# Three score buffers and four term buffers instead of two and five, with the second transpose in bf16 instead of 32-bit

## The chip, the cores and the metric

The kernel runs on one core of a Trainium2 chip. The engines are TensorE (PE, with its weight loads shown as PEld), VectorE (DVE), ScalarE (ACT), GpSimd (POOL) and SyncE (SP), which issues the DMAs. The metric is device time in microseconds of one execution. The median of the kernel before is 1739.27 us, of three runs from 1738.40 to 1739.86 us.

## The reference

Two layers follow each other, with the same weights in both. Each layer is an attention block and a token-mixing MLP, both with a residual:

```python
x = x + _A_ref(_layernorm(x, axis=-1), A_wqkv, A_wo)
x = x + _B_ref(_layernorm(x, axis=-1), B_w1, B_b1, B_w2, B_b2)
x = x + _A_ref(_layernorm(x, axis=-1), A_wqkv, A_wo)
x = x + _B_ref(_layernorm(x, axis=-1), B_w1, B_b1, B_w2, B_b2)
```

x has 2048 tokens of 640 features in bf16. `_A_ref` projects to q, k and v of 32 heads of 20 features, takes a softmax over all 2048 keys of the scores times 20 ** -0.5, multiplies by v and projects with wo. `_B_ref` normalises each token once more and works across tokens: w1 takes the 2048 tokens to 1536, then bias, GELU (tanh form), and w2 takes 1536 back to 2048, with a bias.

## The kernel before

**Attention.** The 32 heads are taken in 8 groups of 4 (`NG`), the queries in 4 blocks of 512, the keys in 16 tiles of 128. A unit is one query block, one head group and one key tile: 512 units a layer, 64 chunks of scores for each (query block, group) pair, which is called a segment. A chunk is the 128 x 512 scores of one head; four of them make a unit. The score matmuls (line 700) use four row tiles of PE, one for each head. The exponential of a chunk is taken in one of two ways:

- ScalarE (`do_exp`, line 887) reads two or three chunks at once from PSUM and writes `P` in bf16. There are four buffers of it (`NP_BUFS`).
- VectorE (`do_J` and `do_T`) makes exp2 out of integers. `do_J` (line 840) scales one chunk from PSUM into 16-bit integers in a buffer `J` that holds the four chunks of a unit. From that buffer `do_T` (line 860) makes five integer terms, each a halving with another constant, which read as bf16 are pieces of the exponential. Their sum is made by PE, which multiplies each of the five terms with v. A term buffer (`TT`) holds one term of one unit, 2048 values in each partition.

The multiplication with v (line 927) uses four column tiles of PE, and adds up over a segment in bank 6 of PSUM. One extra column of v is 1, so that the sums of the softmax come with it.

**Buffers.** `NJ_BUFS` = 2 buffers J and `NT_BUFS` = 5 buffers TT lie one behind the other in one region `JT` of 7 x 4096 bytes in each partition. A J buffer is taken by the first chunk of a unit and is given back when the fifth term has been made; a TT buffer is given back when PE has read its four chunks. In the first query block the last two TT buffers (`NTSV`) are held by saved partial sums, and `begin` leaves the other three free.

**Normalising a segment** (`normalize`). VectorE transposes the sums out of PSUM in blocks of 32 x 32 (line 976, 512 elements of 32 bits), takes the reciprocal of the sums (line 988), GpSimd multiplies (line 1001) into bf16, and VectorE transposes back (line 1011) into `attnT`. Before the change the multiply interleaves pairs of blocks, so that the transpose back moves 256 elements of 32 bits, each a pair of bf16. The output projection (`outproj`, line 1065) undoes the interleaving in the way that it reads its weights: four column tiles of 32 weights with a step of 2.

The last segment of a layer is computed in two halves of 256 queries, which are not interleaved.

**Output projection.** In query blocks 0 to 2 it is made when all 8 groups are there. In the last block it is made in parts: groups 0 to 5 after group 5, then 6 and 7 after group 7. The first part adds the residual into `x1last` (line 1094), a later part adds to it (line 1104).

**What sets the order.** The whole order on every engine is written while the program is built, by a planner. It keeps a clock for each engine, durations for each instruction (such as 600 ns for line 840, 605 for line 860, 720 for line 976), and rings of buffers with the time at which each is free. At each step it lets the engine with the earliest possible piece of work take it. `d_take` gives a unit to VectorE only if a J buffer is to be had and VectorE's clock would be through with it before ScalarE's. Other matmuls (projections, first MLP matmul, output projection) are fills between the attention's matmuls. On the chip each engine runs its instructions in that order and waits for semaphores.

Of the kernel before, what the change touches and what calls it, by code (L numbers as in the profile page):

```python
# [12 lines left out]
F32 = mybir.dt.float32  # L13
# [10 lines left out]
NG = 8  # L24
# [20 lines left out]

TERM_C = term_constants()
NP_BUFS = 4
NJ_BUFS = 2
NT_BUFS = 5
NA_BUFS = 10  # L50
NQ_BUFS = 9
NEARLY0 = 4
# [74 lines left out]
def kernel(  # L127
# [509 lines left out]
    def make_attention(L):  # L637
# [330 lines left out]
        def normalize(qb, g, half, src, ready, from_acc):  # L968
# [4 lines left out]
            def f_tr(start):  # L973
# [1 line left out]
                T1 = sb("T1", [128, w], F32, s1)  # L975
                nc.vector.transpose(out=T1[:], in_=src[:, 0:w])  # L976
                if from_acc:
                    acc["ready"] = start + 720 + LAT_V
                else:
                    sv_open[0] -= 1  # L980
                    if sv_open[0] == 0:
                        for i in range(NT_BUFS - NTSV, NT_BUFS):
                            rTT.give(i, start + 600)
                T1v = T1[:].rearrange("p (c i) -> p c i", i=32)

                def f_rec(start):
                    rden = stat.tile([128, 16], F32, name="rden")[:, 0:w // 32]
                    nc.vector.reciprocal(out=rden, in_=T1v[:, :, DH])  # L988

                    def f_mul(start):  # L990
                        s2 = rT2.take()
                        T2 = sb("T2", [128, w // 32, 32], BF16, s2)
                        eng = nc.vector if final else nc.gpsimd
                        end_ = start + (600 if final else 1450)
                        o_, a_, b_ = T2[:], T1v, rden.unsqueeze(2).to_broadcast([128, w // 32, 32])
                        if half is None:

                            o_ = o_.rearrange("p c i -> p (c i)").rearrange("p (c i b) -> p c b i", b=2, i=32)
                            a_ = T1[:].rearrange("p (c b i) -> p c b i", b=2, i=32)
                            b_ = rden.rearrange("p (c b) -> p c b", b=2).unsqueeze(3).to_broadcast([128, w // 64, 2, 32])  # L1000
                        eng.tensor_tensor(out=o_, in0=a_, in1=b_, op=ALU.mult)  # L1001
                        rT1.give(s1, end_)

                        def f_tr2(start):
                            if (qb, g) not in attnT:
                                aslot[(qb, g)] = rA.take()
                                attnT[(qb, g)] = sb("attnT", [128, 512], BF16, aslot[(qb, g)])
                            o_, i_ = attnT[(qb, g)][:, q0:q1], T2[:].rearrange("p c i -> p (c i)")
                            if half is None:
                                o_, i_ = o_.bitcast(F32), i_.bitcast(F32)  # L1010
                            nc.vector.transpose(out=o_, in_=i_)  # L1011
                            rT2.give(s2, start + 340)
                            on_normal(qb, g, half, start + 340 + LAT_V)
                        push("DVE", 3, end_, 340, f_tr2, ok=lambda: len(rA) > 0 and L.v_left[1] == 0)
                    if final:
                        push("DVE", 0, start + 150, 600, f_mul, ok=lambda: len(rT2) > 0)
                    else:
                        push("POOL", 0, start + 150 + LAT_V, 1300, f_mul, ok=lambda: len(rT2) > 0)
                push("DVE", 1, start + 720, 170, f_rec)
            push("DVE", 0, ready, 720, f_tr, ok=lambda: len(rT1) > 0)  # L1020

        def on_normal(qb, g, half, ready):
            if qb == LASTQB and g == NG - 3 or qb != LASTQB and g == NG - 1:
                for ttl in range(4):
                    load_xin(qb * 4 + ttl)
            if qb == LASTQB:
                gs = {NG - 3: list(range(NG - 2)), NG - 1: [NG - 2, NG - 1]}.get(g)
                if gs:
                    for ttl in range(4) if half is None else (2 * half, 2 * half + 1):
                        for ci in range(2):  # L1030
                            outproj(qb, gs, ttl, ci, ready, partial=True)
            elif g == NG - 1:
                for ttl in range(4):
                    for ci in range(2):
# [11 lines left out]
        def outproj(qb, gs, ttl, ci, ready, partial):  # L1046
# [8 lines left out]
            mms = []  # L1055
            for gi, gg in enumerate(gs):
                def mm(t, gg=gg, gi=gi):
                    at_ = attnT[(qb, gg)]
                    for c in range(4):
                        n = 4 * ttl + c  # L1060
                        if qb == LASTQB and gg == NG - 1:
                            q_ = at_[:, 32 * n:32 * n + 32]
                        else:
                            q_ = at_[:].rearrange("p (c i b) -> p c b i", b=2, i=32)[:, n // 2, n % 2]
                        nc.tensor.matmul(t[32 * c:32 * c + 32, 0:w], lhsT=q_, rhs=wo_pad[:, gg, c0:c1], start=(gi == 0),  # L1065
                                         stop=(gi == len(gs) - 1), tile_position=(0, 32 * c))
                mms.append(mm)

            def on_start(s):
# [39 lines left out]
            def when():  # L1109
# [1 line left out]
            add_fill(mms, 136.0, evac, 65 + 1.05 * w, ready=when if first else ready, pr=NU - NKT + 1 if final else (qb * NG + gs[-1] + 2) * NKT,  # L1111
                     urgent=qb >= LASTQB - 1, on_start=on_start, after=after,
                     ok=(lambda: tt in xin and (partial and L.mm1_left[0] == 0 or not partial and ("ds" in tt_state[tt] or len(rXD) > 0))) if first
                     else (lambda: n_part.get((tt, ci), 0) == 1))

        L.acc, L.pv, L.unassigned, L.pv_total, L.pv_done, L.d_count = acc, pv, unassigned, pv_total, pv_done, d_count
        L.opt_SA, L.do_SA, L.opt_SD, L.do_SD, L.do_PV, L.pv_ready, L.acc_open = opt_SA, do_SA, opt_SD, do_SD, do_PV, pv_ready, acc_open
# [556 lines left out]
```

## Time and profile before

| | us |
|---|---|
| median of three runs | 1739.27 |
| time of the profiled execution | 1739.86 |
| its span | 1738.1 |
| PE busy | 1660.4 (96%) |
| ScalarE busy | 1590.3 (91%) |
| VectorE busy | 1463.7 (84%) |
| GpSimd busy | 183.2 (11%) |

Busy time is the time in which at least one instruction of the engine ran. In the lists of groups each line has the source line, the engine, the operation, the tile written and read, the shapes, how often, then busy time and mean duration in ns, then how long the engine was idle just before such instructions and what ended that. The granted clock of TensorE is 0.994 over the span. The attention of layer 0 ends at about 803 us and that of layer 1 at about 1663 us; in both, query block 1 starts where VectorE makes the ninth first transpose of the layer (239 and 1096 us), block 2 at 422 and 1280 us, block 3 at 613 and 1470 us.

### The profile page before, as it was taken

What the parts mean: (1) busy time and instruction counts of PE and PEld (TensorE: products, weight loads), DVE (VectorE), ACT (ScalarE), POOL (GpSimd) and SP (SyncE); (2) the same over time, 40 slices, a digit from 0 to 9 for tenths busy, and PEclk for the clock granted to TensorE, in tenths of its full rate; (3) what the DMA queues carried; (4) which work ended last, traced back from release to release, by engine and by line L of the source; (5) the groups of instructions that cost most, each with busy time, mean ns of one, the idle gap of its engine ahead of it and who ended that gap; (6) DMA issues with size and microseconds to landing.
All of it is one profiled execution on the core that took longest, in us unless ns stands there. A gap on an engine that the chain in (4) does not pass through costs nothing.

```text
span 1738.1 us, 50479 instructions
## 1 busy us (share of the span) xinstructions
PE 1660.4 (96%) x21922; PEld 640.6 (37%) x21923; DVE 1463.7 (84%) x2613; ACT 1590.3 (91%) x1436; POOL 183.2 (11%) x297
## 2 busy tenths in 40 slices
PE   8999999999999999998999999999999999999989
PEld 3433333323333333335545423332233333333356
DVE  6588999999988889997444699999999888889963
ACT  7899999999999999997598799999999999999950
POOL 3100002000300021001101000210002000300010
PEclk9999999999999999999999999999999999999999
DMA  3200001000121105610522000100002120266133
GB/s 118 29 2 2 2 13 36 1 1 2 52 70 56 38 32 178 191 47 28 162 84 68 15 2 2 39 24 2 2 19 69 56 64 24 78 192 198 63 99 96
DMA packets 103295, 98.06 MB, mean 56 GB/s; under 512 B 45600, under 2 KB 79520, under 8 KB 103072
## 3 DMA queue, kind: packets, MB, share of 16 engines
q1 hardware_dynamic: 99456, 94.82, 17.7%
q8 instruction: 171, 2.80, 0.7%
q0 software_dynamic: 3616, 0.01, 0.3%
q14 instruction: 52, 0.43, 0.1%
HBM read 63.35 MB, written 31.46 MB: 55 GB/s over the span
## 4 chain that ended last, share of the span: by engine, by line
PE 48%; ACT 21%; DVE 19%; issue 9%; DMA 2%; POOL 1%; DVEq 0%; POOLq 0%; SPq 0%; ACTq 0%
ACT P L887 21%; PE pst L700 14%; PE pst L927 13%; PE pst L456 12%; DVE JT L860 7%; DVE JT L840 6%; PE pst L453 5%; PE pst L1065 3%; DVE T_85 L976 1%; PE pst L1483 1%; DMA W<-in_B_w_dram 1%; DVE attnT L1011 1%; DVE QT L463 0%; DMA uacc_74<-W 0%; DVE xs L1094 0%
## 5 line engine op out<-in xcount | busy, mean ns | idle before, releaser
L887 ACT ACTIVATE P<-pst 128x1536 bf16<-128x1536 f32 (+1 forms) x1336 | 1523.5, 1294 | 31.4 <-PE pst L700 15.3
L860 DVE TENSOR_SCALAR JT<-JT 128x2048 uint16<-128x2048 uint16 x945 | 636.0, 706 | 3.9 <-PE pst L927 0.2
L700 PE MATMUL pst<-QT,KT 32*128 32x512 bf16 (+1 forms) x4224 | 589.8, 376 | 36.3 <-ACT P L887 26.5
L840 DVE TENSOR_SCALAR JT<-pst 128x512 uint16<-128x512 f32 x756 | 504.0, 678 | 81.1 <-PE pst L700 78.2
L927 PE MATMUL pst<-P,Vaug 128*32 128x512 bf16 (+1 forms) x3444 | 503.9, 380 | 3.7 <-ACT P L887 1.9
L927 PE MATMUL pst<-JT,Vaug 128*32 128x512 bf16 (+1 forms) x3900 | 464.0, 379 | 4.9 <-DVE JT L860 2.4
L700 PEld LDWEIGHTS <-KT 32*128 32x128 bf16 x4224 | 165.5, 91 | 504.5 <-issue 492.8
L927 PEld LDWEIGHTS <-Vaug 128*32 128x32 bf16 x7344 | 170.9, 94 | 307.1 <-issue 275.6
L1001 POOL TENSOR_TENSOR T_86<-T_85,rden 128x512 bf16<-128x512 f32 x64 | 67.7, 1057 | 1157.1 <-DVE rden L988 1114.9
L1065 PE MATMUL pst<-wo,attnT 128*32 128x320 bf16 x2048 | 108.1, 304 | 7.1 <-DVE attnT L1011 3.9
L1483 PE MATMUL pst<-ident,zw 128*32 128x512 bf16 (+1 forms) x352 | 113.5, 374 | 0.0
L456 PEld LDWEIGHTS <-W 128*32 128x32 bf16 x3384 | 91.0, 96 | 59.8 <-issue 27.7
L456 PE MATMUL pst<-hh,wq 128*32 128x512 bf16 x1232 | 102.2, 381 | 2.2 <-DVE JT L840 1.7
L456 PE MATMUL pst<-hh,wk 128*32 128x512 bf16 x1240 | 95.2, 381 | 1.3 <-DVE JT L840 0.6
L456 PE MATMUL pst<-x1last,W 128*32 128x320 bf16 x1536 | 81.5, 301 | 0.8 <-DVE JT L840 0.4
L1065 PEld LDWEIGHTS <-attnT 128*32 128x32 bf16 x2048 | 51.7, 96 | 49.1 <-issue 26.8
L456 PE MATMUL pst<-attnT,hh 128*32 128x320 bf16 x1196 | 61.4, 300 | 2.5 <-DVE JT L840 0.8
L456 PE MATMUL pst<-JT,W 128*32 128x320 bf16 x1080 | 51.8, 300 | 0.0
L456 PE MATMUL pst<-hh,W 128*32 128x320 bf16 x768 | 43.2, 304 | 5.1 <-DMA W<-in_B_w_dram 3.7
L463 DVE CAST KT<-pst 128x512 bf16<-128x512 f32 x51 | 34.7, 679 | 15.9 <-PE pst L456 14.6
L976 DVE STREAM_TRANSPOSE T_85<-pst 128x512 f32<-128x512 f32 (+1 forms) x58 | 39.9, 688 | 7.0 <-PE pst L927 7.0
L354 POOL TENSOR_SCALAR rt<-mv 128x1 f32<-128x1 f32 x64 | 13.0, 203 | 310.9 <-DVE mv L346 309.9
(92 smaller groups left out, 878.3 us busy)
## 6 DMA issues: line engine op xcount, KB each, us to landing
W<-in_B_w_dram SPq DMA_DIRECT2D x10, 768.0 KB
W<-in_B_w_dram SPq DMA_DIRECT2D x24, 256.0 KB
xs<-in_A_x_dram SPq DMA_DIRECT2D x32, 160.0 KB
x2d<-xs SPq DMA_DIRECT2D x16, 320.0 KB
xs<-x2d SPq DMA_DIRECT2D x16, 320.0 KB
x1d_69<-xs SPq DMA_DIRECT2D x12, 320.0 KB
uacca_72<-W SPq DMA_DIRECT2D x12, 320.0 KB
W<-uacca_72 SPq DMA_DIRECT2D x12, 320.0 KB
```

Source lines behind the costliest of these rows:

```text
L453: nc.tensor.matmul(out_, lhsT=lhsT, rhs=rhs, start=start, stop=stop)
L456: nc.tensor.matmul(out_[32 * c:32 * c + 32], lhsT=lhsT[:, 32 * c:32 * c + 32], rhs=rhs, start=start, stop=stop, tile_position=(0, 32 * c))
L463: nc.vector.tensor_copy(out=out_, in_=in_)
L700: pe(nc.tensor.matmul(dst, lhsT=k_, rhs=q_, start=True, stop=True, tile_position=(32 * j, 0)))
L840: nc.vector.tensor_scalar(out=c["jt"][:, j * 512:(j + 1) * 512], in0=Dt[:], scalar1=SCALE * LOG2E * 256.0, scalar2=127.0 * 256.0, op0=ALU. ...
L860: nc.vector.tensor_scalar(out=tt_[:], in0=c["jt"][:], scalar1=0.5, scalar2=TERM_C[i], op0=ALU.mult, op1=ALU.add)
L887: nc.scalar.activation(out=P[:, 0:n, :].rearrange("p a b -> p (a b)"), in_=St[:, 0:n, :].rearrange("p a b -> p (a b)"), func=ACT.Exp, scal ...
L927: pe(nc.tensor.matmul(dst, lhsT=Vaug[:, n:n + 32], rhs=ap, start=acc["cnt"][j] == 1 and not part, stop=last[j] and (half is None or part = ...
L976: nc.vector.transpose(out=T1[:], in_=src[:, 0:w])
L1001: eng.tensor_tensor(out=o_, in0=a_, in1=b_, op=ALU.mult)
L1065: nc.tensor.matmul(t[32 * c:32 * c + 32, 0:w], lhsT=q_, rhs=wo_pad[:, gg, c0:c1], start=(gi == 0), stop=(gi == len(gs) - 1), tile_position ...
L1483: pe(nc.tensor.matmul(dst[0:32, 0:128 * n], lhsT=zw[:, 0:32], rhs=ident[:].unsqueeze(1).to_broadcast([128, n, 128]), start=not inside, sto ...
```

## The change

Two things change.

First, one of the five TT buffers becomes a third J buffer. The region keeps its size. A unit's chunks can be scaled while two older units still wait for terms; one term fewer can wait for PE. In the first query block the saved sums leave two TT buffers free where they left three.

Second, the interleaving is gone. The multiply writes its blocks in order, the transpose back moves 512 bf16 elements, and the output projection reads dense weights, with one full matmul where attention is over and four column tiles where it isn't. The durations that the planner reckons with are 600 and 150 ns for the first transpose and the reciprocal (720 and 170 before) and 400 ns for the transpose back (340 before). And in the last query block the output projection is made in four parts of two groups each (after groups 1, 3, 5 and 7) instead of two parts of six and two groups; the residual's tiles are loaded after group 1 instead of group 5.

```diff
 NP_BUFS = 4
-NJ_BUFS = 2
-NT_BUFS = 5
+NJ_BUFS = 3
+NT_BUFS = 4
...
                 if from_acc:
-                    acc["ready"] = start + 720 + LAT_V
+                    acc["ready"] = start + 600 + LAT_V
...
-                        o_, a_, b_ = T2[:], T1v, rden.unsqueeze(2).to_broadcast([128, w // 32, 32])
-                        if half is None:
-
-                            o_ = o_.rearrange("p c i -> p (c i)").rearrange("p (c i b) -> p c b i", b=2, i=32)
-                            a_ = T1[:].rearrange("p (c b i) -> p c b i", b=2, i=32)
-                            b_ = rden.rearrange("p (c b) -> p c b", b=2).unsqueeze(3).to_broadcast([128, w // 64, 2, 32])
-                        eng.tensor_tensor(out=o_, in0=a_, in1=b_, op=ALU.mult)
+                        eng.tensor_tensor(out=T2[:], in0=T1v,
+                                                in1=rden.unsqueeze(2).to_broadcast([128, w // 32, 32]), op=ALU.mult)
...
-                            o_, i_ = attnT[(qb, g)][:, q0:q1], T2[:].rearrange("p c i -> p (c i)")
-                            if half is None:
-                                o_, i_ = o_.bitcast(F32), i_.bitcast(F32)
-                            nc.vector.transpose(out=o_, in_=i_)
-                            rT2.give(s2, start + 340)
-                            on_normal(qb, g, half, start + 340 + LAT_V)
-                        push("DVE", 3, end_, 340, f_tr2, ok=lambda: len(rA) > 0 and L.v_left[1] == 0)
+                            nc.vector.transpose(out=attnT[(qb, g)][:, q0:q1], in_=T2[:].rearrange("p c i -> p (c i)"))
+                            rT2.give(s2, start + 400)
+                            on_normal(qb, g, half, start + 400 + LAT_V)
+                        push("DVE", 3, end_, 400, f_tr2, ok=lambda: len(rA) > 0 and L.v_left[1] == 0)
...
-                push("DVE", 1, start + 720, 170, f_rec)
-            push("DVE", 0, ready, 720, f_tr, ok=lambda: len(rT1) > 0)
+                push("DVE", 1, start + 600, 150, f_rec)
+            push("DVE", 0, ready, 600, f_tr, ok=lambda: len(rT1) > 0)
...
-            if qb == LASTQB and g == NG - 3 or qb != LASTQB and g == NG - 1:
+            if qb == LASTQB and g == 1 or qb != LASTQB and g == NG - 1:
...
-                gs = {NG - 3: list(range(NG - 2)), NG - 1: [NG - 2, NG - 1]}.get(g)
-                if gs:
+                if g % 2 == 1:
...
-                            outproj(qb, gs, ttl, ci, ready, partial=True)
+                            outproj(qb, [g - 1, g], ttl, ci, ready, partial=True)
...
-                    at_ = attnT[(qb, gg)]
-                    for c in range(4):
-                        n = 4 * ttl + c
-                        if qb == LASTQB and gg == NG - 1:
-                            q_ = at_[:, 32 * n:32 * n + 32]
-                        else:
-                            q_ = at_[:].rearrange("p (c i b) -> p c b i", b=2, i=32)[:, n // 2, n % 2]
-                        nc.tensor.matmul(t[32 * c:32 * c + 32, 0:w], lhsT=q_, rhs=wo_pad[:, gg, c0:c1], start=(gi == 0),
-                                         stop=(gi == len(gs) - 1), tile_position=(0, 32 * c))
+                    mmul(t[:, 0:w], lhsT=attnT[(qb, gg)][:, ttl * 128:(ttl + 1) * 128],
+                                        rhs=wo_pad[:, gg, c0:c1], start=(gi == 0), stop=(gi == len(gs) - 1))
...
-                     else (lambda: n_part.get((tt, ci), 0) == 1))
+                     else (lambda: n_part.get((tt, ci), 0) == gs[0] // 2))
```

## The prediction

> **What bounds the kernel now.** I read the page's busy shares first, then the chain that ended last, then a table of stages, and last the groups with shapes kept apart.
>
> ```profile
> PE 1660.4 (96%) x21922; PEld 640.6 (37%) x21923; DVE 1463.7 (84%) x2613; ACT 1590.3 (91%) x1436; POOL 183.2 (11%) x297
> PE 48%; ACT 21%; DVE 19%; issue 9%; DMA 2%; POOL 1%; DVEq 0%; POOLq 0%; SPq 0%; ACTq 0%
> ```
>
> No single engine is the bound: three share the chain. So I cut the span where the query blocks of each layer end (at VectorE's first transposes). The columns are microseconds and, for each engine, busy time with its count of instructions.
>
> ```profile
> 0.00:239.00 239.00, 226.38 (x2978) 81.93 (x2979) 188.26 (x353) 220.36 (x205) 27.73 (x52) 0.99 0.12 28
> 239.00:422.50 183.50, 176.91 (x2019) 56.85 (x2018) 181.28 (x313) 182.41 (x161) 21.17 (x28) 1.00 0.04 12
> 422.50:612.70 190.20, 186.25 (x2588) 66.98 (x2591) 167.05 (x290) 188.86 (x167) 19.36 (x28) 1.00 0.17 49
> 612.70:802.80 190.10, 176.23 (x2537) 66.87 (x2529) 177.43 (x317) 184.05 (x162) 24.20 (x38) 1.00 0.33 104
> ...
> 1469.80:1663.20 193.40, 178.62 (x2537) 67.19 (x2529) 177.48 (x318) 184.21 (x162) 24.24 (x38) 0.98 0.41 125
> ```
>
> The reader is to see three kinds of stage. In query block 1 (second line) VectorE is busy 181.3 of 183.5 us and ScalarE 182.4: both full. In block 2 (third line) ScalarE is full (188.9 of 190.2), PE nearly (186.3), and VectorE has 23 us free. In block 3 (fourth line; the last line is layer 1's) VectorE has 12.7 and 15.9 us free and none is quite full. Layer 1's blocks 1 and 2 repeat layer 0's within 0.2 us.
>
> ```profile
> L887 ACT ACTIVATE P<-pst 128x1536 bf16<-128x1536 f32 x668 | 1005.3, 1505 | 27.5 <-PE pst L927 13.2 <-PE pst L700 12.0
> L860 DVE TENSOR_SCALAR JT<-JT 128x2048 uint16<-128x2048 uint16 x945 | 636.0, 706 | 3.9 <-PE pst L927 0.2
> L840 DVE TENSOR_SCALAR JT<-pst 128x512 uint16<-128x512 f32 x756 | 504.0, 678 | 81.1 <-PE pst L700 78.2 <-ACT Vaug L461 0.8
> L976 DVE STREAM_TRANSPOSE T_85<-pst 128x512 f32<-128x512 f32 x54 | 38.1, 705 | 2.6 <-PE pst L927 2.6
> L1011 DVE STREAM_TRANSPOSE attnT<-T_86 128x256 f32<-128x256 f32 x62 | 26.6, 431 | 3.6 <-POOL T_86 L1001 3.5
> L1011 DVE STREAM_TRANSPOSE attnT<-T_86 128x256 bf16<-128x256 bf16 x4 | 1.8, 438 | 0.1
> L1104 DVE TENSOR_TENSOR x1last<-pst,x1last 128x320 f32<-128x320 f32 x16 | 7.3, 480 | 2.3 <-PE pst L1065 2.2
> ```
>
> These are the priced rows. Durations overlap their successors, so what one instruction takes from its engine is the step from start to start, which the timeline shows (start, length, instruction):
>
> ```profile
> 356.94 0.43 DVE L1011 STREAM_TRANSPOSE attnT<-T_86 128x256 f32<-128x256 f32 x1
> 357.30 0.65 DVE L840 TENSOR_SCALAR JT<-pst 128x512 uint16<-128x512 f32 x1
> ...
> 359.07 1.88 DVE L860 TENSOR_SCALAR JT<-JT 128x2048 uint16<-128x2048 uint16 x3
> 360.87 1.28 DVE L840 TENSOR_SCALAR JT<-pst 128x512 uint16<-128x512 f32 x2
> 362.07 0.68 DVE L860 TENSOR_SCALAR JT<-JT 128x2048 uint16<-128x2048 uint16 x1
> ...
> 376.64 0.70 DVE L976 STREAM_TRANSPOSE T_85<-pst 128x512 f32<-128x512 f32 x1
> 377.38 0.25 DVE L988 RECIPROCAL rden<-T_85 128x16 f32<-128x16 f32 x1
> ```
>
> A term (L860) steps 0.60 us, a scaled score chunk (L840) 0.60, the 32-bit second transpose 0.36, the first transpose 0.74. ScalarE's unbroken row of 78 exponentials from 312.59 us takes 88.58 us for 195 chunks, 0.454 us a chunk.
>
> **The change part by part.** The order of work is planned while the program is built, so I compared the two built programs instruction by instruction. Over the whole program ScalarE gets 12 score chunks fewer (3328 for 3340) and VectorE three units more: 12 L840 and 15 L860. VectorE also makes 62 second transposes of 512 bf16 elements where it made 62 of 256 32-bit ones, and 48 partial adds (L1104) where it made 16. SP's queue issues as many DMAs as before, some in another order; the POOL multiply is the same 62 in another output order.
>
> *Second transpose.* The trace has no bf16 transpose of 512. Bounds: 0.43 us (as long as the 32-bit one of 256) and 0.88 (twice the bf16 one of 256). The nearest row is the first transpose, same count of elements, 0.705; and bf16 of 256 takes 438 ns where 32-bit of 256 takes 431, so the time goes by elements. I take 0.705, 0.27 us more: 62 x 0.27 = +17 us on VectorE (bounds 0 and +28).
> [...]
>
> *Partial adds.* 32 more x 0.40 us (step; the mean duration is 0.48) = +13 us on VectorE, all in the two third query blocks. PE's load there is no larger, since the same eight head groups are projected.
>
> *Three more units.* 12 x 0.60 + 15 x 0.60 = +16 us on VectorE, 12 x 0.454 = -5.5 us on ScalarE.
>
> *Terms held in four buffers, scaled scores in three.* L860 stood idle 3.9 us in all, so five buffers hardly made it wait; L840's 81.1 us of idle are 78.2 us of waiting for score matmuls, not for a buffer, and 20.2 of them lie in block 2, where VectorE is not the bound. So neither buffer has a price of its own that I can find beyond the new order. Below: nothing won, or VectorE's free 2.2 us in block 1 won. Above: a fifth term that waits one round of score matmuls (0.33 us, from 572.43 to 572.76 in PE's timeline) for each of block 1's 56 units, 18 us. I take 0, by the 3.9 us row.
>
> *What POOL blocks.* In the trace 32 of the 62 normalisations have a term that starts under the POOL multiply (1.05 us) and is stretched, to 1.17 us in the one at 192.17 us. Laid against the new order, 28 would; about 3 us less for VectorE. I take -1, since most of it falls where VectorE has time; with the multiply's length unchanged (its 256 form took 0.89 us behind a term already running, which gives no other price).
>
> *A plan that is late.* The planner's own durations change with the edit: first transpose 720 to 600 ns (measured step 740), second 340 to 400 (I expect 630 as a step). So the real VectorE falls some 0.4 us further behind its plan at each of 62 normalisations, and the sums' bank, which PE's next group of accumulations needs, comes free 0.14 us later than PE's order reckons with. All of it on PE: 62 x 0.14 = +9; none: 0. Waits of PE for that transpose are 3.7 us today. I take +3. Behind the waiting accumulation on PE stand the next score matmuls, for which ScalarE waits.
>
> By stages, with the step prices (VectorE's sum before and after; ScalarE's chunks):
>
> - Block 0. Layer 0: 185.5 to 189.2 us of VectorE in a stage with 50 us free, chunks equal: 0. Layer 1: ScalarE 4 chunks more (+1.8), VectorE -3, PE some 3 less: +1.
> - Block 1. Chunks equal (400). VectorE 179.4 to 180.4 and to 182.8, with 2.2 us free: +1.0 and +3.4, of which I take +4 together.
> - Block 2. ScalarE 416 to 408 chunks in each layer, -3.6 us. VectorE 160.2 to 171.4 fits into its 23 free us. PE, the next in line, turns between score and column work 18 and 14 times fewer; a turn costs 0.11 us or more (0.33 a round against 0.22 a step in the stream), -2 each. I take -3 each: -6.
> - Block 3. Chunks equal (408). VectorE 172.6 to 183.0 and 182.4: +10 each, into 12.7 and 15.9 us of free time, 3 of which lie in the last 10 us where it waits for the end of attention. Nothing hidden +10, all hidden 0; VectorE reached at most 99% in block 1, and 177.4 + 10.4 is 99% of 190. The cover is nearly gone, and where it is gone, score chunks are read late and PE waits for their bank. I take +3.5 each: +7.
> - The MLP and the end: both hold the same VectorE work (71.6 and 28.0 us); 16 whole matmuls for 64 quarter ones at the end: 0.
>
> Sum: 1 + 4 - 6 + 7 + 3 - 1 = +8. The profiled execution took 1739.86 us (span 1738.1 and 1.8 around it), the slowest of the three runs shown; the median 1739.27 lies 0.6 below. 1739.9 + 8, less that 0.6, is 1747.3; I say 1747.5.
>
> **The rivals.**
> *A: the lighter ScalarE decides (faster).* Place: block 2, and PE's fewer turns in block 3. Price: -3.6 x 2 + 1.8 = -5.4, with some of PE's 2 us in each block 3: 1733. It decides if VectorE's added 10 us in each block 3 vanish in its 12.7 and 15.9 free us and the late plan costs under 2 us. For it: ScalarE is 99% busy in block 2. Against: no stage has fewer chunks but that one, and block 1's VectorE is full.
> *B: gains and losses cancel.* Block 3 and the lateness hidden, block 1 paid: 1 + 4 - 6 - 1 = -2: 1738. For it: idle time of 12 us and more. Against: that idle is spread, and in the two of the 40 slices before 782 us VectorE is busy 41.8 and 41.9 of 43.5 us.
> *C: VectorE binds.* Blocks 1 and 3 pay in full (4.4 + 20.2), PE pays the 9 us of lateness, block 2 gives its 6: +28, 1767; with the term buffers' 18 beyond that. Against: L860's 3.9 us of idle.
> *D: the third buffer does nothing of what it says.* Score chunks already wait for PE, not for a buffer; then the new order is chance and A to C still decide by its counts.
>
> **How the numbers follow.** What can be told from no change is about 0.2%, 3.5 us. The forecast (1743 to 1757) 0.55, C (above) 0.12, B 0.15, A 0.18; D is within them. Slower 0.67, same 0.15, faster 0.18. The range 1733 to 1762 leaves out half of A and the upper two thirds of C. As cases of both signs hold chances, the forecast's own range is 1743 to 1757.
>
> **What would show it.** L1011 with 512 bf16 elements near 705 ns, 62 of them (431 would end that step and put A ahead). L860 960 and L840 768 times. Block 2 some 3 us shorter, block 1 and block 3 longer, with VectorE busy above 98% in block 3. PE's wait at L927 for the first transpose above 3.7 us. L860's idle still small; if it is tens of us, the four term buffers bind. I am wrong if block 3 keeps its 190 us with VectorE's 10 us inside it, or if PE's fewer turns shorten blocks 1 and 3 as well.

## The result and the profile after

The changed kernel takes 1744.97 us (median of four runs, 1743.14 to 1746.77) against 1738.84 us of the kernel before in the same series. The ratio is 1.0036, with a 95% interval from 1.0018 to 1.0053: 6 us slower, 3 to 9. The forecast was 8 us slower (1747.5), so the sum held. Its terms did not all hold: two of them, the one for the buffers and the one for the late plan, were off by 8 to 9 us each, in opposite directions.

The page of the changed kernel: busy time by engine, then the chain that ended last.

```profile
PE 1657.4 (95%) x21950; PEld 641.1 (37%) x21951; DVE 1501.5 (86%) x2675; ACT 1586.3 (91%) x1430; POOL 181.5 (10%) x296
PE 47%; DVE 35%; ACT 11%; issue 6%; POOL 1%; DMA 0%; DVEq 0%; POOLq 0%; SPq 0%; ACTq 0%
```

PE and ScalarE are busy for 3 and 4 us less than before, VectorE for 38 us more. The chain tells more than busy time: VectorE's share of it has gone from 19% to 35%, ScalarE's from 21% to 11%. Work that PE waits for now comes late from VectorE. ScalarE feels it by way of PE: its own waits for VectorE fell from 5.7 to 2.5 us, its waits for PE rose from 69.2 to 75.6 us.

The groups of the changed kernel that answer to the priced rows (count, busy time and mean ns, idle time before):

```profile
L860 DVE TENSOR_SCALAR JT<-JT 128x2048 uint16<-128x2048 uint16 x960 | 645.5, 702 | 5.6 <-PE pst L927 2.2 <-PE pst L456 0.6
L840 DVE TENSOR_SCALAR JT<-pst 128x512 uint16<-128x512 f32 x768 | 511.2, 677 | 57.0 <-PE pst L700 54.2
L1003 DVE STREAM_TRANSPOSE attnT<-T_86 128x512 bf16<-128x512 bf16 x62 | 43.1, 698 | 1.9 <-POOL T_86 L995 1.8
L1088 DVE TENSOR_TENSOR x1last<-pst,x1last 128x320 f32<-128x320 f32 x48 | 22.3, 478 | 1.6 <-PE pst L453 1.1 <-PE pst L456 0.5
```

The transpose back of 512 bf16 elements takes 698 ns; 705 was expected. Terms, chunks and partial adds have the counts that were read off the built order. The terms' idle time is 5.6 us, so four term buffers did not starve VectorE.

The stages, cut at the same first transposes as before (counted in the trace, block 1 starts at the 8th of its layer, not the ninth; us; then busy time and count for PE, PEld, VectorE, ScalarE, GpSimd; then the clock and the DMA):

```profile
0.00:239.80 239.80, 227.33 (x2977) 84.39 (x2978) 191.88 (x357) 220.27 (x204) 27.95 (x52) 0.99 0.12 28
239.80:425.20 185.40, 176.38 (x2011) 56.32 (x2010) 181.79 (x311) 182.65 (x161) 19.50 (x28) 1.00 0.04 12
425.20:616.30 191.10, 186.94 (x2642) 66.19 (x2638) 176.55 (x305) 187.00 (x165) 20.32 (x28) 1.00 0.16 49
616.30:807.40 191.10, 177.52 (x2548) 67.46 (x2540) 186.45 (x337) 183.45 (x162) 25.12 (x36) 0.99 0.33 104
...
1100.70:1288.20 187.50, 177.59 (x2038) 57.30 (x2031) 184.87 (x316) 183.06 (x162) 20.11 (x28) 1.00 0.05 16
1288.20:1478.50 190.30, 185.09 (x2625) 66.60 (x2626) 175.00 (x305) 185.74 (x164) 19.96 (x28) 1.00 0.18 53
1478.50:1666.80 188.30, 175.96 (x2538) 66.20 (x2534) 183.78 (x335) 184.72 (x163) 21.61 (x34) 1.00 0.40 125
```

| stage | before, layers 0 and 1 | after | change |
|---|---|---|---|
| block 1 | 183.5, 183.6 | 185.4, 187.5 | +1.9, +3.9 |
| block 2 | 190.2, 190.1 | 191.1, 190.3 | +0.9, +0.2 |
| block 3 | 190.1, 193.4 | 191.1, 188.3 | +1.0, -5.1 |

Block 1 is longer, as forecast. Block 2 should have become 3 us shorter in each layer and did not, although ScalarE's busy time there fell by 1.9 and 3.0 us. Block 3 of layer 1 is 5 us shorter; in the execution of before, its clock was 0.98 where it is 1.00 here, and it took 3.3 us longer than layer 0's, so part of that difference may belong to the one execution and not to the change. All stages together differ by 3.3 us in these two executions, less than the medians do, so the stages show where time moved but not the whole 6 us.

The waits of PE, before and after (total us, times, longest):

```profile
PE pst L927 <- DVE T_85 L976: 3.7, 9, 0.5
PE pst L456 <- DVE JT L840: 3.9, 14, 1.1
PE pst L700 <- DVE JT L840: 2.5, 9, 0.6
PE pst L1065 <- DVE JT L840: 2.0, 6, 0.6
```

```profile
PE pst L927 <- DVE T_85 L976: 9.6, 22, 1.1
PE pst L456 <- DVE JT L840: 6.8, 22, 0.9
PE pst L700 <- DVE JT L840: 3.9, 10, 0.9
```

The first line is the wait for the bank of the sums, which the first transpose frees: 22 waits where there were 9. In the others, PE waits for VectorE to have read a score chunk out of a bank. The matmuls of the output projection stand at L1065 before (2048, in column tiles) and nearly all at L456 after (1984, in column tiles too), so the three rows of before, 8.4 us, answer to the two of after, 10.7 us. Added up over all rows in which VectorE ends a wait of PE, it is 26.8 us before and 41.8 after.

### The profile page after: what moved, and what is told of

Its sections match the earlier page's. It is cut to its first block, busy times and chain, and to the rows that moved or that the text cites. A ratio compares the mean times of both kernels' runs of the same rounds, so it can differ in the third digit from the quotient of the medians.

```text
span 1741.4 us, 50646 instructions
## 1 busy us (share of the span) xinstructions
PE 1657.4 (95%) x21950; PEld 641.1 (37%) x21951; DVE 1501.5 (86%) x2675; ACT 1586.3 (91%) x1430; POOL 181.5 (10%) x296
## 4 chain that ended last, share of the span: by engine, by line
PE 47%; DVE 35%; ACT 11%; issue 6%; POOL 1%; DMA 0%; DVEq 0%; POOLq 0%; SPq 0%; ACTq 0%
PE pst L456 14%; DVE JT L860 14%; PE pst L700 14%; PE pst L927 13%; DVE JT L840 12%; ACT P L887 10%; PE pst L453 5%; DVE T_85 L976 2%; DVE attnT L1003 2%; PE pst L1467 1%; DVE QT L463 1%; DVE xs L1078 1%; DVE rden L988 1%; DVE W L1230 0%; DVE x1last L1088 0%
## 5 line engine op out<-in xcount | busy, mean ns | idle before, releaser
L860 DVE TENSOR_SCALAR JT<-JT 128x2048 uint16<-128x2048 uint16 x960 | 645.5, 702 | 5.6 <-PE pst L927 2.2
L700 PE MATMUL pst<-QT,KT 32*128 32x512 bf16 (+1 forms) x4224 | 579.4, 376 | 34.4 <-ACT P L887 22.4
L840 DVE TENSOR_SCALAR JT<-pst 128x512 uint16<-128x512 f32 x768 | 511.2, 677 | 57.0 <-PE pst L700 54.2
L927 PE MATMUL pst<-P,Vaug 128*32 128x512 bf16 (+1 forms) x3424 | 511.1, 380 | 5.6 <-DVE T_85 L976 4.2
L927 PE MATMUL pst<-JT,Vaug 128*32 128x512 bf16 (+1 forms) x4000 | 486.4, 376 | 10.3 <-DVE T_85 L976 5.4
L700 PEld LDWEIGHTS <-KT 32*128 32x128 bf16 x4224 | 161.0, 91 | 493.9 <-issue 481.2
L927 PEld LDWEIGHTS <-Vaug 128*32 128x32 bf16 x7424 | 174.5, 94 | 319.8 <-issue 290.1
L456 PE MATMUL pst<-wo,attnT 128*32 128x320 bf16 x1984 | 108.0, 301 | 5.4 <-DVE JT L840 3.9
L456 PEld LDWEIGHTS <-W 128*32 128x32 bf16 x3384 | 90.7, 96 | 59.9 <-issue 31.9
L456 PE MATMUL pst<-hh,wq 128*32 128x512 bf16 x1232 | 101.7, 381 | 2.2 <-DVE JT L840 1.1
L456 PE MATMUL pst<-hh,wk 128*32 128x512 bf16 x1240 | 98.4, 381 | 2.0 <-DVE KT L463 0.6
L456 PE MATMUL pst<-x1last,W 128*32 128x320 bf16 x1536 | 81.7, 301 | 1.2 <-DVE W L1232 0.7
L456 PEld LDWEIGHTS <-attnT 128*32 128x32 bf16 x1984 | 51.4, 96 | 46.9 <-issue 29.8
L456 PE MATMUL pst<-attnT,hh 128*32 128x320 bf16 x1196 | 60.1, 300 | 1.7 <-ACT Vaug L461 0.6
L456 PE MATMUL pst<-JT,W 128*32 128x320 bf16 x1080 | 51.7, 300 | 0.0
L1003 DVE STREAM_TRANSPOSE attnT<-T_86 128x512 bf16<-128x512 bf16 (+1 forms) x66 | 44.9, 682 | 2.0 <-POOL T_86 L995 1.8
L456 PEld LDWEIGHTS <-wq 128*32 128x32 bf16 x1232 | 31.9, 95 | 35.7 <-issue 20.2
```

Of the source, the lines that this page charges most:

```text
L456: nc.tensor.matmul(out_[32 * c:32 * c + 32], lhsT=lhsT[:, 32 * c:32 * c + 32], rhs=rhs, start=start, stop=stop, tile_position=(0, 32 * c))
L700: pe(nc.tensor.matmul(dst, lhsT=k_, rhs=q_, start=True, stop=True, tile_position=(32 * j, 0)))
L840: nc.vector.tensor_scalar(out=c["jt"][:, j * 512:(j + 1) * 512], in0=Dt[:], scalar1=SCALE * LOG2E * 256.0, scalar2=127.0 * 256.0, op0=ALU. ...
L860: nc.vector.tensor_scalar(out=tt_[:], in0=c["jt"][:], scalar1=0.5, scalar2=TERM_C[i], op0=ALU.mult, op1=ALU.add)
L927: pe(nc.tensor.matmul(dst, lhsT=Vaug[:, n:n + 32], rhs=ap, start=acc["cnt"][j] == 1 and not part, stop=last[j] and (half is None or part = ...
L1003: nc.vector.transpose(out=attnT[(qb, g)][:, q0:q1], in_=T2[:].rearrange("p c i -> p (c i)"))
```

## The experiments

Three explanations stood against each other. Theory 1 is the prediction's: VectorE's added work costs where VectorE is full, lateness against the plan costs little, and the buffers nothing. Rival 1: four term buffers are too few. Rival 2: any newly drawn order moves the time by a few us. After the first four runs theory 2 took theory 1's place: what costs is VectorE's lateness against the planned order, and work that the planner reckons with costs less. All ratios are to the kernel before, measured beside each kernel.

### The buffers alone

```diff
 (the kernel before)
-NJ_BUFS = 2
-NT_BUFS = 5
+NJ_BUFS = 3
+NT_BUFS = 4
```

> The kernel before with three score buffers and four term buffers, nothing else. The built order gives ScalarE 3336 chunks (3340 before) and VectorE 4 chunks and 5 terms more. Theory 1 (buffers have no price of their own; what counts is VectorE's load where it is full): by step sums block 1 has 177.0 and 178.8 us of VectorE work against 179.4 before, ScalarE 1.8 us less, so 2 to 4 us faster than before, about 1736. Rival 1 (four term buffers make VectorE wait): L860's idle of 3.9 us grows to 10 us or more and the time to 1744 or above. Rival 2 (any newly drawn order moves the time by a few us either way): within 5 us of before, with stage changes that follow no load.

Measured: 0.9981 [0.9972, 0.9990], 3.3 us faster. The terms' idle time is 5.2 us, so rival 1 falls. The sign and size were theory 1's, but the place was not: layer 1's block 1 went from 183.6 to 185.7 us, and block 2 (187.4 and 189.1) and block 3 of layer 1 (189.5) gave the gain; part of the latter may be the clock's, 1.00 here and 0.98 in the execution of before.

### The transpose alone, in the same order

```diff
 (the kernel before; planner durations unchanged)
-                        if half is None:
-
-                            o_ = o_.rearrange("p c i -> p (c i)").rearrange("p (c i b) -> p c b i", b=2, i=32)
-                            a_ = T1[:].rearrange("p (c b i) -> p c b i", b=2, i=32)
-                            b_ = rden.rearrange("p (c b) -> p c b", b=2).unsqueeze(3).to_broadcast([128, w // 64, 2, 32])
...
-                            if half is None:
-                                o_, i_ = o_.bitcast(F32), i_.bitcast(F32)
...
-                        if qb == LASTQB and gg == NG - 1:
-                            q_ = at_[:, 32 * n:32 * n + 32]
-                        else:
-                            q_ = at_[:].rearrange("p (c i b) -> p c b i", b=2, i=32)[:, n // 2, n % 2]
+                        q_ = at_[:, 32 * n:32 * n + 32]
```

> The kernel before with the multiply, the transpose back and the projection's weights not interleaved, all planner durations as before: the same instructions in the same order on every engine, 62 of them longer by 0.27 us on VectorE. Theory 1 (paid where VectorE is full): 2 us in each block 1, 1 to 2 in each block 3, nothing in blocks 0 and 2: 4 to 8 us slower than before, 1743 to 1747. If all 62 were paid: 17 us slower. Rival 1 and rival 2 (buffers, or the drawn order, made the 6 us): no change, within 2 us of before.

Measured: 1.0056 [1.0044, 1.0069], 9.7 us slower. The order on every engine is the one of before, so nothing was drawn anew and rival 2 is out for this term. It is more than theory 1's 4 to 8, and it lies in stages where theory 1 had nothing. The stages of this kernel, with layer 1's block 0 from its first transpose on as the last line:

```profile
0.00:241.00 241.00, 226.91 (x2978) 82.19 (x2979) 190.16 (x354) 220.69 (x205) 27.72 (x52) 0.98 0.11 28
241.00:425.80 184.80, 177.91 (x2017) 56.41 (x2017) 182.82 (x313) 183.10 (x161) 21.06 (x28) 1.00 0.04 12
425.80:616.50 190.70, 186.44 (x2588) 66.67 (x2591) 168.68 (x289) 188.90 (x167) 18.82 (x28) 1.00 0.17 49
616.50:808.10 191.60, 178.10 (x2537) 66.96 (x2530) 179.50 (x317) 184.49 (x162) 24.18 (x38) 0.99 0.33 104
...
975.60:1102.80 127.20, 123.06 (x1621) 41.13 (x1620) 112.63 (x188) 117.91 (x106) 7.35 (x7) 1.00 0.01 2
```

That last stage in the kernel before:

```profile
970.40:1096.10 125.70, 122.59 (x1621) 41.05 (x1620) 110.88 (x188) 117.39 (x106) 7.37 (x7) 1.00 0.01 2
```

Layer 0's block 0 is 2.0 us longer with 51 us of VectorE free, block 1 1.3, block 2 0.5 with 22 us free, block 3 1.5. In blocks 0 and 3 the clock is 0.01 lower than before, so part of their share can be the clock's; layer 1's block 0 is 1.5 us longer at a clock of 1.00 in both, with 15 us free. Idle time in a stage hid only part of it: of 62 x 0.27 = 17 us on VectorE, 10 came through. The author's reading is that in a fixed order the instruction behind a late one is late too, until VectorE's next idle moment, and whoever waits for it in that stretch stands still. Of this the traces show that PE's waits for VectorE to read a score chunk grew from 8.4 to 12.3 us, and all its waits for VectorE from 26.8 to 32.0. Its waits for the first transpose did not grow (3.7 and 3.4 us).

### The changed kernel without the buffers

```diff
 (the changed kernel)
-NJ_BUFS = 3
-NT_BUFS = 4
+NJ_BUFS = 2
+NT_BUFS = 5
```

> The changed kernel with two score buffers and five term buffers again. ScalarE has 3324 chunks, VectorE's step sums in block 1 are 178.6 and 178.0 us (180.4 and 182.8 in the changed kernel). Theory 1: 3 to 6 us faster than the changed kernel in block 1, the rest as there: 1739 to 1742. Rival 1 (term buffers): the whole loss that is not the transpose's goes, L860 idle falls to 4 us. Rival 2: anything from 1738 to 1750, in stages that the loads do not point to.

Measured: 1.0089 [1.0075, 1.0103], 15.5 us slower than before and 9 slower than the changed kernel. Theory 1 and rival 1 had both expected it to be faster. The third score buffer helps, and the rest of the change costs some 15 us. PE's waits in this kernel:

```profile
PE pst L456 <- DVE JT L840: 10.0, 25, 1.7
PE pst L700 <- DVE JT L840: 5.7, 16, 0.8
PE pst L927 <- DVE T L976: 4.9, 13, 0.9
```

The plan is as late as the changed kernel's, yet the bank of the sums accounts for 4.9 us only; the waits for score chunks are 15.7 us.

### True durations

```diff
 (the changed kernel)
-                    acc["ready"] = start + 600 + LAT_V
+                    acc["ready"] = start + 740 + LAT_V
...
-                            rT2.give(s2, start + 400)
-                            on_normal(qb, g, half, start + 400 + LAT_V)
-                        push("DVE", 3, end_, 400, f_tr2, ok=lambda: len(rA) > 0 and L.v_left[1] == 0)
+                            rT2.give(s2, start + 630)
+                            on_normal(qb, g, half, start + 630 + LAT_V)
+                        push("DVE", 3, end_, 630, f_tr2, ok=lambda: len(rA) > 0 and L.v_left[1] == 0)
...
-                push("DVE", 1, start + 600, 150, f_rec)
-            push("DVE", 0, ready, 600, f_tr, ok=lambda: len(rT1) > 0)
+                push("DVE", 1, start + 740, 170, f_rec)
+            push("DVE", 0, ready, 740, f_tr, ok=lambda: len(rT1) > 0)
```

> The changed kernel whose planner reckons with 740, 170 and 630 ns for first transpose, reciprocal and transpose back, as measured, where it has 600, 150 and 400. ScalarE has 3336 chunks (3328). Theory 1 with the plan's lateness as priced (about 3 us, up to 9): PE's waits at L927 for the first transpose fall from 7 us to 4 or less and the time is 3 to 6 us below the changed kernel, 1739 to 1742, although ScalarE has 3.6 us more. If lateness costs nothing: as the changed kernel or up to 4 us slower by ScalarE's chunks. Rival 2: within 5 us of the changed kernel with no link to PE's waits.

Measured: 0.9972 [0.9960, 0.9983], 4.9 us faster than before and 11 faster than the changed kernel, with the same long transposes, the same partial adds and 8 chunks more on ScalarE. The waits of PE in this kernel:

```profile
PE pst L927 <- DVE T L976: 3.9, 10, 1.1
PE pst L456 <- DVE JT L840: 3.2, 14, 0.4
PE pst L700 <- DVE JT L840: 2.4, 7, 0.6
```

They are back at the level of before: 10 waits for the bank of the sums instead of 22. The sum of PE's waits for VectorE is 25.0 us. The two blocks 2 of this kernel:

```profile
421.90:610.00 188.10, 184.62 (x2621) 67.28 (x2618) 171.93 (x298) 186.64 (x165) 21.12 (x28) 1.00 0.17 50
1276.50:1465.50 189.00, 184.25 (x2609) 66.15 (x2609) 173.62 (x301) 186.08 (x165) 18.63 (x28) 1.00 0.18 53
```

They are 3.2 us shorter together than before, so about half of the 6 us that the prediction expected there appears when the plan is true.

### Four parts alone

```diff
 (the kernel before)
-            if qb == LASTQB and g == NG - 3 or qb != LASTQB and g == NG - 1:
+            if qb == LASTQB and g == 1 or qb != LASTQB and g == NG - 1:
...
-                gs = {NG - 3: list(range(NG - 2)), NG - 1: [NG - 2, NG - 1]}.get(g)
+                gs = [g - 1, g] if g % 2 == 1 else None
...
-                     else (lambda: n_part.get((tt, ci), 0) == 1))
+                     else (lambda: n_part.get((tt, ci), 0) == gs[0] // 2))
```

> The kernel before with the last block's projection in four parts of two groups: 32 partial adds more, 6.4 us of VectorE in each block 3, chunks and terms unchanged, ScalarE's order the same. Theory 2 (what is in the planner's durations is fitted in, only what it doesn't know of costs): 0 to 3 us slower than before. Theory 1 (every microsecond on VectorE in block 3 is paid by half): 6 us slower. If loading the residual earlier helps the end: up to 3 us faster.

Measured: 1.0033 [1.0021, 1.0044], 5.7 us slower. That is theory 1's size, not theory 2's: of the 13 us of partial adds nearly half is paid, although the planner knows their length. In its profiled execution (span 1740.7 us) only layer 0's block 3 is longer, 193.3 for 190.1 us; layer 1's is 192.0 for 193.4, with the clock at 1.00 for 0.98. It is one pair, and 5.7 us is also the size of the largest difference between redrawn orders below. As it stands it speaks against theory 2's second half, that planned work costs less.

### A late plan alone

```diff
 (the kernel before)
-                    acc["ready"] = start + 720 + LAT_V
+                    acc["ready"] = start + 600 + LAT_V
...
-                            rT2.give(s2, start + 340)
-                            on_normal(qb, g, half, start + 340 + LAT_V)
-                        push("DVE", 3, end_, 340, f_tr2, ok=lambda: len(rA) > 0 and L.v_left[1] == 0)
+                            rT2.give(s2, start + 130)
+                            on_normal(qb, g, half, start + 130 + LAT_V)
+                        push("DVE", 3, end_, 130, f_tr2, ok=lambda: len(rA) > 0 and L.v_left[1] == 0)
...
-                push("DVE", 1, start + 720, 170, f_rec)
-            push("DVE", 0, ready, 720, f_tr, ok=lambda: len(rT1) > 0)
+                push("DVE", 1, start + 600, 150, f_rec)
+            push("DVE", 0, ready, 600, f_tr, ok=lambda: len(rT1) > 0)
```

> The kernel before, 32-bit transpose and two score buffers kept, whose planner is told 600, 150 and 130 ns for first transpose, reciprocal and transpose back: by the steps measured before (740, 171, 360) it is then late by 0.39 us at each normalisation, as the changed kernel's is, with no longer instruction. The order gives ScalarE 3320 chunks, 20 fewer, 9 us of its time. Theory 2 (lateness against the plan is what costs): 6 to 12 us slower than before, 1743 to 1749, PE's and ScalarE's idle time up. Theory 1 (the work costs where VectorE is full, lateness a little): VectorE's sums in block 1 are as before, block 2 and 3 have room; 0 to 6 us faster by the chunks.

Measured: 1.0047 [1.0035, 1.0059], 8.2 us slower, with the short transpose and 20 chunks fewer on ScalarE. Theory 1 had it 0 to 6 us faster, and falls. The chain and the waits show the same picture as in the changed kernel. First the chain of the kernel with the late plan, then PE's waits in it:

```profile
PE 45%; DVE 31%; ACT 15%; issue 8%; POOL 1%; DMA 1%; DVEq 0%; POOLq 0%; SPq 0%; ACTq 0%
```

```profile
PE pst L927 <- DVE T L976: 7.2, 15, 1.2
PE pst L456 <- DVE JT L840: 4.6, 13, 0.6
PE pst L700 <- DVE JT L840: 6.0, 19, 0.6
```

VectorE's share of the chain is 31% (19% before), and PE's waits for the first transpose have doubled (7.2 us for 3.7).

One rival goes along with every late plan. A planner that takes VectorE to be faster also gives it more units: 20 chunks more here, 8 to 12 more in the other late plans than in the same kernels with true durations, and VectorE is busy for 11 to 19 us more. The stages of this run speak against that as the whole cause. Layer 0's block 2 took most of the added work (167.1 to 176.5 us of VectorE) and is 0.3 us longer; the two blocks 1, where VectorE is full, have 1.2 and 0.7 us less of its work and are 0.4 and 1.1 us longer. How much of the 8.2 us is the added work's share is not shown. In what follows, the cost of a late plan includes it.

### True durations with two score buffers

This is the kernel with true durations, with `NJ_BUFS` = 2 and `NT_BUFS` = 5.

> The changed kernel with true durations (740, 170, 630) and two score, five term buffers: the fourth corner of buffers by plan. ScalarE 3336 chunks as with three buffers. If the third score buffer helps by itself: 6 to 9 us slower than with three buffers and true durations, 1738 to 1741. If it only takes up what a late plan brings (the slack of one more unit): within 3 us of that kernel, 1730 to 1735. Chance of the drawn order: anything between.

Measured: 1.0030 [1.0019, 1.0041], 5.2 us slower than before and 10 slower than with three score buffers. ScalarE has 3336 chunks in both. So the third score buffer does not only take up what a late plan brings; it helps a true plan as much.

### The short transpose, three score buffers and true durations

```diff
 (the kernel before)
-NJ_BUFS = 2
-NT_BUFS = 5
+NJ_BUFS = 3
+NT_BUFS = 4
...
-                    acc["ready"] = start + 720 + LAT_V
+                    acc["ready"] = start + 740 + LAT_V
...
-                            rT2.give(s2, start + 340)
-                            on_normal(qb, g, half, start + 340 + LAT_V)
-                        push("DVE", 3, end_, 340, f_tr2, ok=lambda: len(rA) > 0 and L.v_left[1] == 0)
+                            rT2.give(s2, start + 360)
+                            on_normal(qb, g, half, start + 360 + LAT_V)
+                        push("DVE", 3, end_, 360, f_tr2, ok=lambda: len(rA) > 0 and L.v_left[1] == 0)
...
-                push("DVE", 1, start + 720, 170, f_rec)
-            push("DVE", 0, ready, 720, f_tr, ok=lambda: len(rT1) > 0)
+                push("DVE", 1, start + 740, 170, f_rec)
+            push("DVE", 0, ready, 740, f_tr, ok=lambda: len(rT1) > 0)
```

> The kernel before (32-bit transpose, two parts) with three score and four term buffers and 740, 170, 360 ns in the planner. ScalarE 3332 chunks, VectorE 28 us less than the changed kernel with true durations. Theory 2 and the buffers' own gain: below both kernels, 1728 to 1733. If the true-durations kernel was fast by its four parts or by its draw: as with buffers alone, 1734 to 1737.

Measured: 1724.80 us, 0.9925 [0.9913, 0.9937]: 13 us faster than before, and faster than both kernels of this study. Its chain:

```profile
PE 43%; ACT 30%; DVE 13%; issue 12%; DMA 1%; POOL 1%; SPq 0%; DVEq 0%; POOLq 0%; ACTq 0%
```

Next to PE the chain now follows ScalarE, and VectorE has fallen to 13%. PE waits 2.2 us for the first transpose. The kernel with true durations, which has the long transposes and the four parts beside the same buffers, was 4.9 us faster than before; so in this pair those two parts of the change still cost 8 us, of 30 us of added work on VectorE. The same two kernels with nudged durations, below, show nothing of it (10.1 and 10.6 us faster than before), so that cost is not told from a redrawn order.

### How much a newly drawn order moves the time

The planner draws another order for the smallest change of a duration. Four kernels differ from others of this study by 10 to 20 ns in the first transpose and the transpose back.

The kernel before with 740, 170, 360 ns:

> The kernel before with 740, 170, 360 ns in its planner instead of 720, 170, 340: 40 ns a normalisation less late, 2.5 us in the whole program. ScalarE 3332 chunks, 8 fewer (3.6 us). Theory 2 (lateness, by the 11 us that 0.39 us cost): 1 to 5 us faster than before, 1732 to 1736; the buffers are then worth 7 to 11 us beside the run with three score buffers and these durations. Rival 2 (a newly drawn order moves the time by itself): as far as 8 us faster, and the buffers worth only 4.

Measured: 0.9987 [0.9977, 0.9996], 2.3 us faster, in theory 2's range.

The fastest kernel with 760, 170, 380 ns:

> The fastest kernel (32-bit transpose, three score buffers) with 760, 170, 380 ns in its planner where it had 740, 170, 360. The durations are now a little above the measured steps. Rival 2 is measured here: by theory 2 alone the time stays within 2 us of that kernel, 1723 to 1727; if the draw of the order matters, it moves by 4 us or more in either direction, 1718 to 1732.

Measured: 0.9942 [0.9926, 0.9959], 10.1 us faster than before: 3 us behind the fastest by the ratios, whose intervals overlap.

The kernel with true durations, at 760, 170, 650 ns:

> The changed kernel with 760, 170, 650 ns where the true-durations run had 740, 170, 630. ScalarE 3340 chunks, 4 more. Theory 2 alone: within 3 us of that run, 1730 to 1735. If the draw matters: 4 us or more away from it.

Measured: 0.9939 [0.9924, 0.9954], 10.6 us faster than before, 5.7 away from the run that it was derived from, although ScalarE has 4 chunks more. That is a draw, as rival 2 said.

The changed kernel with 610, 150, 410 ns:

> The changed kernel with 610, 150, 410 ns where it has 600, 150, 400: 20 of its 390 ns of lateness gone. ScalarE 3332 chunks, 4 more. Theory 2 alone: within 2 us of the changed kernel, 1742 to 1746. If the draw matters: 4 us or more away, 1735 to 1752, in which case the 6 us of the change itself are of the size of a draw.

Measured: 1.0049 [1.0034, 1.0064], 8.5 us slower than before, 2.3 beyond the changed kernel, which is within the intervals.

Of these four differences the 5.7 us is clear of noise; the 2.3 us of the kernel before just is, and theory 2 had forecast it. So a redrawn order moves the time by up to 6 us here, in four trials, and rival 2 is real. One pair of kernels that differ in their order by a few us proves little. What stands is what several pairs agree on (us, from the ratios times 1738):

| pair | slower one | faster one | difference |
|---|---|---|---|
| late and true plan, three score buffers | +6.2 | -4.9 | 11 |
| the same, both nudged | +8.5 | -10.6 | 19 |
| late and true plan, two score buffers | +15.5 | +5.2 | 10 |
| late plan and plan of before, short transpose | +8.2 | 0 | 8 |
| two and three score buffers, kernel before | 0 | -3.3 | 3 |
| the same, 740, 170, 360 ns | -2.3 | -13.0 | 11 |
| the same, late plan, long transpose | +15.5 | +6.2 | 9 |
| the same, true plan, long transpose | +5.2 | -4.9 | 10 |

Both effects have one sign in four pairs each, and all but one of the eight differences are larger than the largest draw. The pairs share kernels, so they are not eight independent measurements. The traces go the same way: PE's waits for VectorE add up to 35.7 to 41.8 us in the four kernels with a late plan and to 22.8 to 33.1 us in the other ten (32.0 in the one with the transpose alone, whose long transposes outrun its plan too).

The four corners with the long transposes and four parts then add up. With a true plan and two score buffers they cost 5.2 us; a late plan adds 10 or 11, and the third score buffer takes 9 or 10 away.

## Why the prediction was right, and where not

The total was right: slower, by 6 us where 8 were forecast. Step by step:

**The length of the transpose** was right: 698 ns for 705. The row of 256 elements decided it. 256 bf16 elements took 438 ns and 512 took 698, which is 1.02 ns for each further element; the 32-bit rows (431 and 705 ns) give 1.07 ns. So 16-bit elements went hardly faster than 32-bit ones: in these four rows of transposes the time went by elements and not by bytes.

**Block 1** was right in sign: +4 forecast, +5.8 in the profiled pair. Its reason, VectorE's load where it is full, is not shown: with true durations layer 0's block 1 took 181.5 us (183.5 before) and layer 1's 187.4 (183.6 before).

**"VectorE 160.2 to 171.4 fits into its 23 free us"** failed: block 2 was to give 6 us and gave none (+0.9 and +0.2). The transpose alone, in the same order, showed why: work that the order did not know of was paid even beside free time (+2.0 us in layer 0's block 0, +0.5 in block 2). With true durations the same block took 188.1 and 189.0 us, so about half of the expected gain was there; it was gone with the late plan.

**"A plan that is late ... I take +3"** was the right mechanism at the wrong size. The bounds were 0 and 9; measured 8 to 11 in three pairs, and 19 in the fourth, with the units that a late planner moves to VectorE counted in. (By its own numbers the bound was 7: the plan of before was already 0.02 us late for the bank, so the change adds 0.12 us at each of 62, and 0.35 us for the three steps together.) The bound above was too low as well, since it counted only the bank of the sums, and PE waits for late score reads too: over the profile of before the waits grew by 5.9 us at the first transpose and by 2.3 us in the rows of L840.

**"Neither buffer has a price of its own that I can find"** failed in size: the third score buffer was worth 3 to 11 us, beyond the 2.2 us that were granted as a gain. The term buffers cost nothing that shows, as said. The argument was that score chunks wait for score matmuls and not for a buffer. That is what the row says, but the planner gives VectorE a new unit only when a buffer is to be had, so a missing buffer appears as a score matmul that was planned late. That link is read from the code; no wait in the profiles proves it. With the buffers alone, L840's idle time is 81.5 us, as before (81.1), and the chunk counts hardly differ (3336 and 3336 in the pair with true durations). Part of the gain can be seen at PE: in the three pairs where the third buffer gave 9 to 11 us, PE's waits for score chunks fell by 2.6 to 5.0 us (such as 10.5 to 5.6 with true durations); in the pair with 3 us they did not fall (8.4 and 8.9). How it earns the rest stays open.

**The partial adds** were counted as VectorE's work in block 3, and by themselves cost 5.7 us, near half of their 13 us, in one pair and no more than a draw can do. **Block 3's +7** was +1.0 and -5.1 in the profiled pair. Layer 1's cannot be judged, since its clock differs (0.98 before, 1.00 after). Layer 0's (0.99 after 1.00) is the sign that the prediction named for being wrong: the block kept nearly its 190 us with 9.0 us more of VectorE's work inside it, busy 97.6% of the time where more than 98% was expected.

So the forecast held by luck: an unpriced gain (the buffers, 9 us) stood against an underpriced loss (lateness, 8 us more than taken). The terms without these two came to 1 + 4 - 6 + 7 - 1 = +5, and the kernel with neither, true plan and two score buffers, was 5.2 us slower than before; but blocks 2 and 3 did not do what their terms said, so that agreement is one of sums too. In the rivals' terms, C's mechanism was at work (VectorE's share of the chain 35%), held back by a gain that no rival contained. D, "the third buffer does nothing of what it says", is refuted in its result.

## What to carry to other kernels

In this kernel, where the order on each engine is fixed in advance, VectorE's idle time hid only part of the work that the plan did not know of (10 of 17 us came through): price such work by what waits behind it, and give the planner the measured steps, start to start, before judging any other change. A row that says "waits for a matmul" need not clear a buffer, if the matmul is itself only planned when the buffer is free, as the code has it here: 78.2 of L840's 81.1 us of idle time were such waits, and the third score buffer was worth 3 to 11 us all the same. And before believing a few us of such a kernel, change a duration by 20 ns and see how far the time moves by itself (2.3 to 5.7 us here).

## What the runs showed that had not been expected

Without any longer instruction, telling the planner 0.39 us too little for each normalisation (0.04 before) cost 8.2 us, though it took 20 chunks (9 us) off ScalarE; they went to VectorE, whose busy time rose by 17 us. A nudge of 10 or 20 ns in two planned durations moved the time by 2.3 to 5.7 us, of which only the largest is clearly a draw. And the three good parts together (short transpose, three score buffers, true durations) gave 1724.8 us, 13 us below the kernel before, of which the buffers alone gave 3.3 and the durations alone 2.3; the rest came only from both, or from a lucky draw: the nudged version of the same kernel keeps 10 of the 13.
